# Score blocks of three groups in one stretch of 64-row work, with the second MoE product in 64-row halves between them

## The chip, the cores and the metric

The kernel runs on one core of a Trainium2 chip. The metric is the device time of one execution in microseconds. The engines are named as in the profile: PE is TensorE's matmuls and PEld its weight loads, DVE is VectorE, ACT is ScalarE, POOL is GpSimd, and SP is the engine whose queue issues DMAs here.

## The reference

A sliding-window attention is followed by a two-layer network with a squared ReLU. The batch is 8, there are 8 heads, 576 positions and a head dimension of 64; the window reaches 32 positions to either side.

```python
scores = scale * np.matmul(q, k.transpose(0, 1, 3, 2))
scores = np.where(np.abs(pos[:, None] - pos[None, :]) <= 32, scores, -1e9)
attn   = softmax(scores)
x = np.matmul(attn, v)          # as 4608 tokens x 512
h = x @ w_in                    # 512 x 2048
r = np.maximum(h, 0.0)
out = (r * r) @ w_out           # 2048 x 512, float32
```

## The kernel before

**Units of work.** The 4608 tokens are cut into 24 groups G of 192 queries (three groups, g = 0 to 2, for each batch b), and into 36 output blocks u of 128 tokens.

For a group, `scores` (S) multiplies k by q for all eight heads and for the two key windows w = 0 and 1. The head dimension is 64, so each matmul uses only 64 of the array's 128 rows: heads with an even number use rows 0 to 63, the odd ones rows 64 to 127, and they alternate. The sixteen matmuls of a group fill `AT`, 2048 columns in four PSUM banks. ACT takes the exponential of each half of AT (line 573), DVE multiplies it with a mask (line 578) into one of three `PT` buffers, `pv` (P) multiplies that with v (line 606) back into AT, and DVE divides and clears (lines 625 to 634). `xturn` transposes the result into `XT`, a ring of 1536 tokens, by DMA transposes on SP's queue (lines 701 and 704).

The first MoE product is `mm1` (A, line 721): 192, 256 or, from token 2048 on, 512 tokens at a time, by parts of the 2048 hidden features; ACT takes the relu out of the two PSUM tiles `HT` (line 727) and DVE the square into the ring `GT` (line 730). The second product is `mm2` (B, line 741): for a block u sixteen matmuls of 128 rows by 512 columns, in four segments, accumulate in `OUTP[u % 2]`; ACT evicts it (line 751) and stores it. The last block has a form of its own (`mm2_last`).

**Inputs.** Loads of q, k and v (`load_qk`, `load_v`, lines 378 and 427) go through POOL's queue and convert to bf16. From batch 2 on, q and k are transposed by DMAs on SP's queue (`turn_dma`, line 509), in chunks of 128 positions. Each load is recorded with `after=self.moe`: it waits for the score or first-product block that was recorded last before it.

**Order.** Nothing is emitted in the order of the code. `Prog.rec` collects operations with their dependences, an estimated duration and a key. One key unit is 64 tokens of the first product: A's key is its place in tokens, S of group G has 3G − `LEAD`, loads come a further `AHEAD` before, turns 3 units before S, and B of block u stands at 2u + `LAG`. The operations are recorded in the order of their keys. `Prog.schedule` then plays a list schedule: each engine takes, of the operations whose inputs are there by its estimates, the one with the lowest key. The DMA rings are played too, with an allowance (`slack`) added to the landing of each transfer. `Prog.emit` writes each engine's instructions in that order with the semaphore waits. On the chip each engine then works strictly in this order.

Of the kernel before, what the change touches and what calls it, by code (L numbers as in the profile page):

```python
# [18 lines left out]
RING = 1536  # L19
NV, NRAW = 6, 6  # L20
NTURN = 2
NXT = 3
LEAD = 13.0
LAG = 9.0
AHEAD = 9.0
TISS = 1340
# [37 lines left out]
PIECES = {"k": ((0, 1), (2, 3), (4,)), "q": ((0, 1), (2,), (3, 4))}  # L64
KC = ((0, 224), (224, 192), (416, 160))


class Op:
    __slots__ = ("eng", "fn", "deps", "order", "inc", "val", "sem", "dma", "dur", "key", "i",
                 "succ", "left", "ready", "start", "end", "lat", "move", "name", "slack")  # L70


class Prog:
# [5 lines left out]
    def __init__(self, nc):  # L79
        self.nc = nc  # L80
        self.ops = []
        self.writer = {}
        self.readers = {}

    def rec(self, eng, fn, reads=(), writes=(), dma=None, dur=100, key=0.0, move=0, name="", after=None, slack=0, war=()):
# [5 lines left out]
        op.slack = slack  # L91
        op.lat = self.LAT[eng]
# [24 lines left out]

    def schedule(self):
        ops = self.ops
        for op in ops:  # L120
            op.succ, op.left, op.ready = [], 0, 0
        for op in ops:
# [13 lines left out]
        order = ["POOL", "SP", "ACT"]  # L136
        now = spent = 0.0

        def done(op, end):
            for s in op.succ:  # L140
                s.ready = max(s.ready, end if op in s.deps or op.eng != s.eng else free[op.eng])
                s.left -= 1
                if not s.left:
                    heapq.heappush(wait[s.eng], (s.ready, s.i, s))
# [27 lines left out]
        while True:  # L172
            best = None
            for e in engs:
                if pool[e]:
# [13 lines left out]
            if serve(t):  # L189
                continue  # L190
            while wait[e] and wait[e][0][0] <= t:
                _, i, op = heapq.heappop(wait[e])
                heapq.heappush(pool[e], (op.key, i, op))
            first = pool[e][0]
# [10 lines left out]
            else:  # L205
                op.end = t + op.dur + op.lat
                done(op, op.end)
        assert len(out) == len(ops)
        self.length = max(o.end for o in out)
        at = free["PE"] = 1500  # L210
        for op in sorted((o for o in out if o.eng == "PE"), key=lambda o: o.start):
            gap = min(op.start, WARM, self.idle_end.start) - at
            one = 430 if at < 5000 else 230
            for k in range(int((gap - 60) // one)):
                w = Op()
                w.eng, w.fn, w.dma, w.deps, w.i = "PE", self.idle, None, {self.idle_on}, op.i
                w.inc, w.val, w.sem, w.start, w.end, w.dur, w.key = False, None, None, at + one * k, 0, one, -99
                w.name = "idle"
# [4 lines left out]
    def emit(self):  # L223
        nc = self.nc
        engs = {"PE": nc.tensor, "ACT": nc.scalar, "DVE": nc.vector, "POOL": nc.gpsimd, "SP": nc.sync}
        for op in self.ops:
            for d in op.deps:
                if d.dma is None and not (d.eng == "PE" and op.eng == "PE"):
                    d.inc = True
        sems = {e: nc.alloc_semaphore(f"s_{e}") for e in engs}  # L230
        count = {e: 0 for e in engs}
# [5 lines left out]
        for op in self.ops:  # L237
            e = engs[op.eng]
            need = {}
            for d in op.deps:  # L240
                if d.dma is None and d.eng == "PE" and op.eng == "PE":
                    continue
                need[d.sem] = max(need.get(d.sem, 0), d.val)
            for s, v in need.items():
# [26 lines left out]
class Gen:  # L271
# [5 lines left out]
    def alloc(self):  # L277
# [13 lines left out]
        self.E = [sb(f"e{i}", [128, 1024], BF16) for i in range(2)]  # L291
        self.PT = [sb(f"pt{i}", [128, 8, 128], BF16) for i in range(3)]
        self.RS = [sb(f"rs{i}", [128, 8], F32) for i in range(4)]
# [223 lines left out]
    def scores(self, G, ws):  # L517
        b, g = divmod(G, 3)
        i = b % 2
        kt, qt = self.KT[i], self.QT[i]  # L520
        key = 3 * G - LEAD + 0.3 * ws[0]
        a = 192 * g
# [38 lines left out]
        if G < NBIAS:  # L561
            rd += [t for w in ws for t in tags[w]]
        self.moe = self.p.rec("PE", f, reads=rd, writes=[t for w in ws for t in tags[w]], key=key, dur=190 + 235 * len(ws),
                              name=f"S{G}{'AB'[ws[-1]]}")
        for w in ws:
            n = 2 * G + w
            sc = self.AT[:, 1024 * reg[w]:1024 * reg[w] + 1024]
            e_, pt = self.E[n % 2], self.PT[n % 3]
            if G < NBIAS:
                self.p.rec("ACT", lambda e, pt=pt, sc=sc: e.activation(pt[:].rearrange("p h q -> p (h q)"), sc, ACTF.Exp, scale=0.125),  # L570
                           reads=tags[w], writes=[("pt", n % 3)], key=key, dur=act(1024), name=f"X{G}{'AB'[w]}")
                continue
# [5 lines left out]
            self.p.rec("DVE", lambda e, pt=pt, ee=ee, mb=mb: e.tensor_tensor(pt[:], ee, mb, ALU.mult),  # L578
                       reads=[("e", n % 2), ("mask", mi)], writes=[("pt", n % 3)], key=key, dur=dve(1024),
                       name=f"M{G}{'AB'[w]}")  # L580

    def pv(self, G, w):
# [5 lines left out]
        vt, pt, avp = self.V[G % NV], self.PT[n % 3], self.AT  # L588
        hi, lo = [self.half(2 * reg, x) + self.half(2 * reg + 1, x) for x in (1, 0)]


        def f(e):
            if w and G < NDUP:
                for h in range(8):
                    x, y = divmod(h, 4)
                    c = c0 + 512 * x + 65 * y
                    e.matmul(avp[:, c:c + 65], self.PT[(n - 1) % 3][:, 4 * (h % 2) + h // 2, :], vt[:, 0, h, 0:65], start=(y == 0),
                             stop=True, skip_group_check=True)
# [10 lines left out]

        rd = [("v", G % NV, w), ("vset", G % NV), ("pt", n % 3), "zz"]  # L610
        if G % 3 != 1:
# [3 lines left out]
        if G < NDUP and w:  # L615
            rd += [("pt", (n - 1) % 3), ("v", G % NV, 0)]
        self.p.rec("PE", f, reads=rd + (lo if w and G >= NDUP else []), writes=hi + lo, key=key, dur=260 + 160 * (w and G < NCLR) + 260 * (w and G < NDUP),
# [18 lines left out]
    def xturn(self, G):  # L636
        xa, xb = self.XA[G % 3], self.XB[G % 3]
        key = 3 * G - LEAD + 0.5
        r = 192 * G % RING
# [94 lines left out]
    def mm2(self, u, seg, key):  # L734
# [4 lines left out]
        def f(e):  # L739
            for d in range(4 * seg, 4 * seg + 4):  # L740
# [4 lines left out]
                       + ([f"outp{u % 2}"] if seg else []),  # L745
                       writes=[f"outp{u % 2}"], key=key, dur=864, name=f"B{u}.{seg}")
        if u == 1 and seg == 0 and not XTD:
            self.p.idle_end = o
# [34 lines left out]
    def build(self):  # L783
# [33 lines left out]
        for g in (1, 2, 4, 5):  # L817
            self.copy_v(g, K + 7 if g < 3 else 3 * g - LEAD - AHEAD)
        todo = []

        def at(key, f, *a):
            todo.append((key, len(todo), f, a))

        for G in range(NG):
            b, g = divmod(G, 3)
            if b > 1:
                key = 3 * G - LEAD - AHEAD
                for t in "kq":
# [3 lines left out]
                if g and G < NVR:  # L832
                    key = 3 * G - LEAD - 0.5 if G >= VCS else key
                    at(key + 0.01, self.copy_v, G, key - VKEY if G >= VCS else key)
            for t in "kq":
                key = 3 * G - LEAD - (0.6 if b < NTURN else 3)
                for c in (g,) if b < NTURN else PIECES[t][g]:
                    at(key, self.turn_pe if b < NTURN else self.turn_dma, t, b, c, key)
            for ws in ((0,), (1,)) if G < NSPLIT else ((0, 1),):
                at(3 * G - LEAD + 0.3 * ws[0], self.scores, G, ws)  # L840
# [58 lines left out]
```

## Time and profile before

| | us |
|---|---|
| median of 3 runs | 303.6 |
| lowest and highest | 303.34, 303.64 |
| profiled execution, span from its first to its last instruction | 301.1 |
| PE busy | 291.9 |
| PEld busy | 170.9 |
| DVE busy | 166.5 |
| ACT busy | 160.7 |
| POOL busy | 102.4 |

Of the profiled execution's own time the profile gives the span; the median of the runs is 2.5 us longer, for what lies around the span. The ends of matmuls are modelled, so their starts are what to read. A few matmul records are missing from the trace: a row of a timeline with x3 where its neighbours have x4 is as long as they are.

### The profile page before, as it was taken

Reading aid. Unit: us, or ns where it says so; the run is one execution under the profiler, and the core shown is the slowest. Engines: PE = TensorE matmul, PEld = TensorE weight load, DVE = VectorE, ACT = ScalarE, POOL = GpSimd, SP = SyncE. Lnnn points to the kernel's source line nnn. Section 1 sums busy time; section 2 is a strip of 40 time slices with the busy share of each in tenths; the row PEclk is TensorE's granted clock in tenths of the full one; section 3 lists DMA queues with packets and bytes.
Section 4 is the critical chain, followed back from the end, with each engine's and each line's share of the span. In section 5 each row is a group of like instructions: output and inputs, shape, how many; then the busy total and the mean of one; then the engine's idle time right before and its main releaser. Section 6 shows DMA issues by size and latency. Waiting matters only on the chain.

```text
span 301.1 us, 6232 instructions
## 1 busy us (share of the span) xinstructions
PE 291.9 (97%) x2394; PEld 170.9 (57%) x2431; DVE 166.5 (55%) x385; ACT 160.7 (53%) x250; POOL 102.4 (34%) x131
## 2 busy tenths in 40 slices
PE   7899999999999999999999999999999999999996
PEld 2578866846677777764444445445444444444445
DVE  5898785726766766664378756666456322222100
ACT  3587834826567646644656666455636443443312
POOL 8993335406543543654065454330000000000000
PEclk9999999999999999999999999999999999999999
DMA  9999999999998999999999999994121201000112
GB/s 167 176 206 183 196 178 176 168 163 208 175 158 138 141 160 191 147 157 177 199 152 135 166 162 143 199 168 101 54 50 49 60 35 37 35 35 36 37 70 105
DMA packets 160060, 39.83 MB, mean 132 GB/s; under 512 B 149408, under 2 KB 155552, under 8 KB 160032
## 3 DMA queue, kind: packets, MB, share of 16 engines
q0 software_dynamic: 105824, 17.93, 86.1%
q1 hardware_dynamic: 48880, 12.14, 28.4%
q10 hardware_dynamic: 5328, 9.37, 8.9%
q8 instruction: 19, 0.31, 0.4%
q14 instruction: 9, 0.07, 0.1%
HBM read 36.70 MB, written 9.44 MB: 153 GB/s over the span
## 4 chain that ended last, share of the span: by engine, by line
PE 87%; DMA 7%; POOL 3%; issue 1%; ACT 1%; DVE 0%; ACTq 0%; POOLq 0%
PE ht L721 41%; PE outp L741 38%; DMA w<-in_moe_w_in_dram 5%; PE at L606 4%; PE at L548 3%; DMA xt<-xa 2%; POOL v L427 1%; POOL w L440 1%; PE at L469 1%; PE ht L766 1%; PE outp L766 1%; POOL kpair L410 1%; POOL qpair L410 1%; ACT rt L727 0%; ACT oe L751 0%
## 5 line engine op out<-in xcount | busy, mean ns | idle before, releaser
L721 PE MATMUL ht<-xt,w 128*128 128x256 bf16 (+2 forms) x886 | 142.4, 302 | 1.7 <-DMA xt<-xa 0.5
L741 PE MATMUL outp<-w,gt 128*128 128x512 bf16 x535 | 134.3, 379 | 1.4 <-issue 0.2
L727 ACT ACTIVATE rt<-ht 128x512 bf16<-128x512 f32 (+1 forms) x152 | 86.4, 577 | 90.8 <-PE ht L721 85.7
L721 PEld LDWEIGHTS ht<-xt,w 128*128 128x128 bf16 x896 | 80.8, 98 | 43.8 <-DMA xt<-xa 1.0
L730 DVE TENSOR_TENSOR gt<-rt 128x512 bf16<-128x512 bf16 (+1 forms) x152 | 61.3, 408 | 65.0 <-ACT rt L727 63.2
L741 PEld LDWEIGHTS outp<-w,gt 128*128 128x128 bf16 x560 | 52.3, 98 | 56.0 <-ACT oe L751 1.1
L378 POOL DMA_DIRECT2D kraw<-in_k_dram x30 | 25.3, 850 | 95.2 <-PE at L548 76.5
L573 ACT ACTIVATE e<-at 128x1024 bf16<-128x1024 f32 x46 | 44.8, 1021 | 11.2 <-PE at L548 11.1
L578 DVE TENSOR_TENSOR pt<-e,mask 128x1024 bf16<-128x1024 bf16 x46 | 31.5, 691 | 24.7 <-ACT e L573 24.6
L427 POOL DMA_DIRECT2D v<-in_v_dram x48 | 38.4, 822 | 0.0
L751 ACT ACTIVATE oe<-outp 128x512 f32<-128x512 f32 x35 | 21.1, 602 | 24.1 <-PE outp L741 24.1
L378 POOL DMA_DIRECT2D qraw<-in_q_dram x30 | 25.5, 860 | 0.0
L606 PEld LDWEIGHTS at<-v,pt 128*128 128x128 bf16 x384 | 18.0, 98 | 10.0 <-DVE at L634 1.8
L606 PE MATMUL at<-v,pt 128*128 128x65 bf16 x384 | 20.1, 194 | 0.5 <-ACT pt L570 0.5
L628 DVE TENSOR_TENSOR xb<-at,rs 128x512 bf16<-128x512 f32 x24 | 16.6, 690 | 1.1
L628 DVE TENSOR_TENSOR xa<-at,rs 64x512 bf16<-64x512 f32 x24 | 16.7, 695 | 0.8
L548 PEld LDWEIGHTS at<-qt,kt 64*128 64x128 bf16 x384 | 10.8, 94 | 8.3 <-issue 7.5
L548 PE MATMUL at<-qt,kt 64*128 64x128 bf16 x384 | 15.2, 217 | 0.1
L625 DVE RECIPROCAL rs<-at 64x8 f32<-64x8 f32 (+1 forms) x48 | 10.0, 209 | 9.5 <-PE at L606 7.8
L634 DVE MEMSET at<- 64x520 f32 x23 | 11.3, 492 | 3.7 <-DVE xa L628 2.9
L434 DVE COPY v<-v 64x512 bf16<-64x512 bf16 x16 | 5.8, 366 | 6.9 <-PE ht L721 5.8
L773 DVE COPY oe<-ht 128x128 f32<-128x128 f32 x1 | 0.3, 291 | 14.7 <-PE ht L766 14.7
(67 smaller groups left out, 82.1 us busy)
## 6 DMA issues: line engine op xcount, KB each, us to landing
out_dram<-oe ACTq DMA_DIRECT2D x35, 256.0 KB, 3.8
kraw<-in_k_dram POOLq DMA_DIRECT2D x24, 128.0 KB, 5.6
qraw<-in_q_dram POOLq DMA_DIRECT2D x24, 128.0 KB, 5.9
w<-in_moe_w_in_dram POOLq DMA_DIRECT2D x4, 512.0 KB, 10.6
v<-in_v_dram POOLq DMA_DIRECT2D x16, 128.0 KB, 7.3
w<-in_moe_w_out_dram POOLq DMA_DIRECT2D x4, 512.0 KB, 18.9
v<-in_v_dram POOLq DMA_DIRECT2D x16, 96.0 KB, 6.7
v<-in_v_dram POOLq DMA_DIRECT2D x16, 64.0 KB, 5.8
```

The source lines that it names most:

```text
L378: self.p.rec("POOL", lambda e: e.dma_start(raw[0:n, x % 2, :].rearrange("p (h d) -> p h d", h=8), s), writes=[("raw", t, x // 2, x % 2)], ...
L427: self.p.rec("POOL", lambda e, j=j, lo=lo, hi=hi, k0=k0: e.dma_start(vt[lo - k0:hi - k0, j, :, 0:64], self.v[b, :, lo:hi, :].rearrange("h ...
L548: mm = e.matmul(sc[:, 512 * par + 128 * j:512 * par + 128 * j + 128], kt[r:r + 64, j, k0:k0 + 128], q, start=G >= NBIAS, stop=True, skip_g ...
L573: self.p.rec("ACT", lambda e, e_=e_, sc=sc: e.activation(e_[:], sc, ACTF.Exp, scale=0.125), reads=tags[w], writes=[("e", n % 2)], key=key, ...
L578: self.p.rec("DVE", lambda e, pt=pt, ee=ee, mb=mb: e.tensor_tensor(pt[:], ee, mb, ALU.mult), reads=[("e", n % 2), ("mask", mi)], writes=[( ...
L606: mm = e.matmul(avp[:, c:c + 65], pt[:, 4 * (h % 2) + h // 2, :], vt[:, w, h, 0:65], start=(w == 0 and y == 0), stop=True, skip_group_chec ...
L628: self.p.rec("DVE", lambda e: e.tensor_tensor(x[r0:128, :].rearrange("p (x y c) -> p x y c", x=2, y=4), av[:, :, :, 0:64], rb, ALU.mult), ...
L721: mm = e.matmul(ht[:, n * x:n * x + n], self.W1[:, ft, 128 * d:128 * d + 128], self.XT[:, ft, r:r + n], start=(ft == 0), stop=(ft == 3))
L727: self.p.rec("ACT", lambda e: e.activation(rt[:, 0:c], ht[:, 0:c], ACTF.Relu), reads=[f"ht{k % 2}"], writes=[("rt", k % 4)], key=key, dur= ...
L730: self.p.rec("DVE", lambda e: e.tensor_tensor(gt[:, d0:d0 + len(ds), r:r + n], rr, rr, ALU.mult), reads=[("rt", k % 4)], writes=[("gt", s, ...
L741: mm = e.matmul(op[:], gt[:, d, r:r + 128], self.W2[:, d, :], start=(d == 0), stop=(d == 15))
L751: self.p.rec("ACT", lambda e: e.activation(oe, op[:], ACTF.Copy), reads=[f"outp{u % 2}"], writes=[("oe", u % 4)], key=key, dur=act(512), n ...
```

## The change

For batches 5, 6 and 7 (groups 15 to 23) the three score blocks of a batch are put on PE as one unbroken chain, with two half blocks H between them: S(G), H0, S(G+1), H1, S(G+2). The two H together are the second product of two whole output blocks u and u+1. H0 multiplies, for each of the 16 parts of the hidden features, rows 0 to 63 for block u and rows 64 to 127 for block u+1; H1 does the other two halves. Each H has 32 matmuls of 64 rows by 512 columns. Each accumulates into OUTP[u % 2] and OUTP[(u+1) % 2] at once, and H1 waits by a semaphore for the end of H0 (`fence`).

In the planner, the first S of a chain is taken when the inputs of all three groups are known to be there within 500 ns, and when two blocks u and u+1 are found that have not begun, whose inputs are there and whose PSUM tiles are free or will be within 500 ns (`fill`); the eight B operations of these blocks are then dropped (`dead`). Until this is so, other work with a higher key goes first. A chain is taken without H (its S then stand singly) when the first product has come to 6 units before the first group's own place, or 20 us after its inputs were there.

`PT` gets seven buffers for three. The keys move for all groups: LEAD 13 to 14, LAG 9 to 9.5, AHEAD 9 to 9.5, and `SOONER` shifts loads and turns of batches 4 to 7. Groups in a chain have their keys 0.75 units apart in place of 3, so their loads, turns and xturn come earlier by up to some 5 units.

```diff
-LEAD = 13.0
-LAG = 9.0
-AHEAD = 9.0
+LEAD = 14.0
+LAG = 9.5
+AHEAD = 9.5
...
+NPT = 7
+CHAINS = {15: 3, 18: 3, 21: 3}
+CSTEP = 0.75
+CEARLY = 12.0
+CHOLD = 12.0
+CLAST = 6.0
+READY = 500
+PATIENCE = 20000
+SOONER = {4: (1, 1.5), 5: (-1.5, 1), 7: (-0.5, 1.5), 6: (2, 2)}
...
     def schedule(self):
...
+        def known(deps, t):
+            return all(d.end is not None and d.end <= t + READY for d in deps)
...
+        def fill(op, t):
+            u = min((u for u, b in self.blocks.items() if b[0].end is None), default=None)
+            if u is None or u + 1 not in self.blocks:
+                return None
+            both = self.blocks[u] + self.blocks[u + 1]
+            deps = {d for b in both for d in b.deps | b.order if d not in both}
+            if not known(deps, t):
+                return None
...
+            seq = [ops[0], op.chain[1], ops[1]] + op.chain[2:]
...
+            return seq
...
+                    if op.chain:
+                        if known({d for y in op.chain for d in y.data}, t):
+                            run = fill(op, t) or []
+                            op.since = t if op.since is None else op.since
+                        if run or at >= op.urge + CHOLD - CLAST or op.since is not None and t > op.since + PATIENCE:
+                            break
+                    elif not (op in opens and any(at >= h[2].urge for h in held if h[2].chain) and spare(t) < 3):
+                        break
...
     def emit(self):
...
+            for d in op.fence:
+                need[d.sem] = max(need.get(d.sem, 0), d.val)
...
     def scores(self, G, ws):
-        key = 3 * G - LEAD + 0.3 * ws[0]
+        key = self.pos(G) - LEAD + 0.3 * ws[0]
...
-            e_, pt = self.E[n % 2], self.PT[n % 3]
+            e_, pt = self.E[n % 2], self.PT[n % NPT]
...
+    def half_block(self, u, kind):
+        gt, w2 = self.GT, self.W2
+        def f(e):
+            for d in range(16):
+                for x in range(2):
+                    v = u + (x + kind) % 2
+                    r, r0 = 128 * v % RING, 64 * x
+                    mm = e.matmul(self.OUTP[v % 2][:], gt[r0:r0 + 64, d, r:r + 128], w2[r0:r0 + 64, d, :], start=kind == 0 and d == 0,
+                                  stop=kind == 1 and d == 15, skip_group_check=True)
+            return mm
+        return f
+
+    def pos(self, G):
+        x = self.chained.get(G, 0)
+        return 3 * (G - x) + CSTEP * x
+
+    def chain(self, G0, n):
+        ops = [self.scores(G0 + x, (0, 1)) for x in range(n)]
+        ops[0].chain, ops[0].urge = ops, 3 * G0 - CHOLD
+        for x in range(n):
+            for w in range(2):
+                self.pv(G0 + x, w)
+            self.xturn(G0 + x)
 
     def pv(self, G, w):
-        key = 3 * G - LEAD + 0.3 * w + 0.1
-        reg = 1 if NBIAS <= G < NSPLIT or G < NDUP and w else 0
+        key = self.pos(G) - LEAD + 0.3 * w + 0.1
+        reg = self.chained[G] % 2 if G in self.chained else 1 if NBIAS <= G < NSPLIT or G < NDUP and w else 0
...
     def build(self):
...
+            pos = self.pos(G)
             if b > 1:
-                key = 3 * G - LEAD - AHEAD
+                key = pos - LEAD - AHEAD - SOONER.get(b, (0, 0))[0]
...
-                key = 3 * G - LEAD - (0.6 if b < NTURN else 3)
+                key = pos - LEAD - (0.6 if b < NTURN else 3 + SOONER.get(b, (0, 0))[1])
...
+            if G in self.chained:
+                if G in CHAINS:
+                    at(3 * G - CEARLY, self.chain, G, CHAINS[G])
+                continue
```

More of the change, by code (lines that the diff above doesn't have):

```diff
@@ L65 @@
 KC = ((0, 224), (224, 192), (416, 160))
+NPT = 7
[7 more added lines that the diff above has]
+SOONER = {4: (1, 1.5), 5: (-1.5, 1), 7: (-0.5, 1.5), 6: (2, 2)}
 class Op:
     __slots__ = ("eng", "fn", "deps", "order", "inc", "val", "sem", "dma", "dur", "key", "i",
-                 "succ", "left", "ready", "start", "end", "lat", "move", "name", "slack")
+                 "succ", "left", "ready", "start", "end", "lat", "move", "name", "slack", "chain", "inner", "dead",
+                 "data", "urge", "since", "fence")
 class Prog:
@@ L91, in rec @@
         op.slack = slack
+        op.chain, op.inner, op.dead, op.data, op.urge, op.since, op.fence = None, False, None, (), None, None, ()
         op.lat = self.LAT[eng]
@@ L137, in schedule, with spare @@
         now = spent = 0.0
+        run, at = [], -99.0
+        opens = {b[0] for b in self.blocks.values()}
+        def known(deps, t):
+            return all(d.end is not None and d.end <= t + READY for d in deps)
+        def spare(t):
+            n = 0
+            for u in sorted(self.blocks):
+                both = self.blocks[u]
+                if both[0].end is None:
+                    if not known({d for b in both for d in b.deps if d not in both and d.eng != "ACT"}, t):
+                        return n
+                    n += 1
+            return n
+        def fill(op, t):
[6 more added lines that the diff above has]
+                return None
+            ops = []
+            for kind in range(2):
+                h = Op()
+                h.eng, h.fn, h.dma, h.deps, h.order, h.i, h.key = "PE", self.half_block(u, kind), None, set(), set(), op.i, op.key
+                h.inc, h.val, h.sem, h.dur, h.lat, h.name = False, None, None, 3450, op.lat, f"H{u}.{kind}"
+                h.succ, h.left, h.ready, h.end, h.dead, h.chain, h.fence = [], 0, 0, None, None, None, ()
+                ops.append(h)
+            ops[1].fence = ops[:1]
+            ops[0].deps = deps
+            for b in both:
+                b.dead = ops[1]
+            ops[1].succ = both
+            op.dur = 560
+            seq = [ops[0], op.chain[1], ops[1]] + op.chain[2:]
+            for x in op.chain[1:]:
+                x.inner, x.dur = True, 450
+            seq[-1].dur += 100
+            return seq
         def done(op, end):
@@ L174, in schedule @@
             for e in engs:
-                if pool[e]:
+                while pool[e] and pool[e][0][2].dead:
+                    heapq.heappop(pool[e])
+                while wait[e] and wait[e][0][2].dead:
+                    heapq.heappop(wait[e])
+                if e == "PE" and run:
+                    if run[0].left:
+                        continue
+                    t = max(free[e], run[0].ready)
+                elif pool[e]:
                     t = free[e]
@@ L226, in emit @@
         for op in self.ops:
+            op.deps = {d.dead or d for d in op.deps}
             for d in op.deps:
@@ L819, in build @@
         todo = []
+        self.chained = {G + x: x for G, n in CHAINS.items() for x in range(n)}
+        p.half_block = self.half_block
         def at(key, f, *a):
```

80 lines of the change are left out of this document (63 added, 17 removed).

## The prediction

> **What bounds the kernel now.** I read the page first (busy time, slices, chain), then the groups by line, the stages, the waits, and the timeline around one score block.
>
> ```profile
> span 301.1 us, 6232 instructions
> PE 291.9 (97%) x2394; PEld 170.9 (57%) x2431; DVE 166.5 (55%) x385; ACT 160.7 (53%) x250; POOL 102.4 (34%) x131
> PE 87%; DMA 7%; POOL 3%; issue 1%; ACT 1%; DVE 0%; ACTq 0%; POOLq 0%
> 24.00:72.00 48.00, 47.18 (x510) 34.21 (x515) 31.06 (x72) 27.73 (x46) 18.62 (x24) 1.00 1.83 181
> 140.00:172.00 32.00, 31.58 (x231) 15.38 (x234) 21.65 (x46) 19.20 (x30) 15.20 (x19) 1.00 1.64 161
> 200.00:230.00 30.00, 29.68 (x211) 14.45 (x214) 16.17 (x36) 16.79 (x26) 0.00 (x0) 1.00 0.43 71
> PE ht L721 <- DMA xt<-xa: 0.5, 1, 0.5
> ```
>
> TensorE is busy 97% of the span and makes up 87% of the chain that ended last. In the three stages (columns: stretch, its length, then busy us of PE, PEld, DVE, ACT, POOL, the granted clock, DMA share, GB/s) it lacks 0.8 us between 24 and 72 us, 0.4 us between 140 and 172, and 0.3 us between 200 and 230, at a clock of 1.00. DVE and ACT are half empty. After the opening the longest wait of TensorE for another unit is one of 0.5 us. So from about 24 us on, a microsecond taken off TensorE's queue is a microsecond off the span, as long as nothing new holds the queue; and work moved between other engines is worth nothing. The change edits TensorE's queue in batches 5 to 7 (score blocks of groups 15 to 23, those from 148.8 to 226.5 us), so I look at one such block, S18, with its neighbours:
>
> ```profile
> 173.12 1.03 PE L741 MATMUL outp<-w,gt 128*128 128x512 bf16 x4
> 173.98 1.03 PE L721 MATMUL ht<-xt,w 128*128 128x512 bf16 x3
> 174.85 1.03 PE L741 MATMUL outp<-w,gt 128*128 128x512 bf16 x4
> 175.81 0.62 PE L548 MATMUL at<-qt,kt 64*128 64x128 bf16 x16
> 176.36 1.04 PE L721 MATMUL ht<-xt,w 128*128 128x512 bf16 x4
> 177.23 1.03 PE L741 MATMUL outp<-w,gt 128*128 128x512 bf16 x4
> 178.09 1.03 PE L721 MATMUL ht<-xt,w 128*128 128x512 bf16 x4
> 178.96 0.42 PE L606 MATMUL at<-v,pt 128*128 128x65 bf16 x8
> 179.22 1.02 PE L741 MATMUL outp<-w,gt 128*128 128x512 bf16 x4
> L548 PE MATMUL at<-qt,kt x384: 212/216/227, 9.7 to 226.9; 64*128 64x128 bf16 x192
> L548 PEld LDWEIGHTS at<-qt,kt 64*128 64x128 bf16 x384 | 10.8, 94 | 8.3 <-issue 7.5 <-ACT qt L497 0.4 <-DVE gt L730 0.2
> ```
>
> A row's second number runs to the modelled end of its last matmul, so the starts are what to read. Four 512-column matmuls take 0.86 us from start to start whatever line follows (177.23 to 178.09): 0.216 each, and a change of line or of output costs nothing. (One row shows x3 for lack of a record; its length is that of four.) Only the score block is different. From 174.85 to its start are 0.96 us, 0.10 more than four matmuls need; to the start of the next block are 0.55 us. Inside it sixteen matmuls of 128 columns on 64 rows start within 0.62 less one duration of 0.216, so every (0.62 − 0.216) / 15 = 0.027 us, two per 0.054, which is what 128 columns take at 0.216 for 512: both halves of the array run at once, and their weight loads (94 ns each, 10.8 / 384 = 28 ns of unshared time) keep up. At that rate the block needs 16 × 0.027 = 0.43 us. It takes 0.10 + 0.55 = 0.65, and the block after it another 0.01 (0.87 for 0.86). So entering and leaving 64-row work costs 0.65 + 0.01 − 0.43 = 0.23 us per block.
>
> **The change, part by part.**
>
> *Switches.* Nine score blocks in batches 5 to 7 now pay 9 × 0.23. Chained as S, H, S, H, S with the H also on 64 rows, a batch enters and leaves once: six of nine switches go, 6 × 0.23 = 1.36 us, all of it on TensorE's queue. This is the one term that is there by design.
>
> *Half blocks.* Per chain, blocks u and u+1 (32 matmuls of 128 rows, 32 × 0.216 = 6.91 us) become two H of 32 matmuls of 64 rows by 512 columns. No row shows these. Nearest is the score block itself: 0.027 us for 128 columns is 0.108 for 512, 32 × 0.108 = 3.46 per H, 6.91 for two: no difference, and I take that. Two bounds above it: if of each pair of weight loads one step of 0.027 were exposed, 96 pairs (3 chains × 2 × 16) would cost 2.6 us; if a full load of 0.094, 9.0 us. Below zero I see nothing: TensorE already runs a column per 0.42 ns in both shapes.
>
> Here the Trainium skill speaks against the change (TensorE: Matmul & The Clock Gate, Part 3, "What overlaps and what doesn't"): a weight load overlaps matmuls in flight only when its row group differs, which would make every pair wait for its loads. The trace does not bear it out for the score block, at 0.027 us per matmul with 94 ns loads; by the page the sum would end at the 9.0 us above, not at zero. The same page (Part 3, "Measured speedup vs the span model") has four row tiles of 512 columns at 3.07 times, not 4; the score block's two tiles run at the full factor of two.
>
> *The fence between the two H.* H1 starts only when H0's last matmul has signalled; behind that wait stand H1, the last score block and everything later on TensorE. ACT started 0.04 us after a recorded matmul end (rows below: 176.43, which is 175.81 + 0.62, then 176.47), and a 512-column matmul is recorded with 0.38 us, so the signal is there about 0.42 us after the last start; S(G+1) between them covers 0.22 + 0.43 = 0.65. Cost nothing; uncovered, as when that block goes first, up to 0.2 × 3 = 0.6.
>
> *Waits for ACT inside a chain.* S(G+1) overwrites the PSUM that S(G)'s two exponentials read.
>
> ```profile
> 175.91 0.60 ACT L751 ACTIVATE oe<-outp 128x512 f32<-128x512 f32 x1 [0.21 <-PE outp L741]
> 176.47 1.02 ACT L573 ACTIVATE e<-at 128x1024 bf16<-128x1024 f32 x1
> 177.39 1.02 ACT L573 ACTIVATE e<-at 128x1024 bf16<-128x1024 f32 x1
> 178.29 0.60 ACT L727 ACTIVATE rt<-ht 128x512 bf16<-128x512 f32 x1
> 177.52 0.69 DVE L578 TENSOR_TENSOR pt<-e,mask 128x1024 bf16<-128x1024 bf16 x1 [1.36 <-ACT e L573]
> 178.44 0.69 DVE L578 TENSOR_TENSOR pt<-e,mask 128x1024 bf16<-128x1024 bf16 x1 [0.22 <-ACT e L573]
> ```
>
> They end at 178.41, 2.60 us after the block's start. H0 covers 0.43 + 3.46 = 3.89 us, so even two more items of 0.60 ahead on ACT (3.80) stay hidden. After the chain the cover is thinner: two evictions (0.60 each) and two exponentials (0.92 apart), 3.0 us of ACT, stand before the relu of the next MoE blocks. TensorE has two first-product blocks for the two free PSUM tiles (1.73), then second-product blocks of u+2 once the first eviction is over. I take nothing; with no block ready it is 3.0 − 1.7 = 1.3 per chain, 3.9 in all. On DVE six masks (0.69 each, 4.1 us) fall into the 8.2 us of a chain, fewer than it has free. The second-product values (P, 0.26 us from 178.96 to 179.22) and the division and clearing behind them keep their count and place on DVE; the seven pt buffers, more than the six a chain fills, mean that no mask waits for P.
>
> *Loads, turns and the planner's keys.* Key units pass at (175.81 − 148.79) / 9, 3.0 us each, counting S15 to S18. Before, every load of group G is issued behind S(G−3), 9 units ahead.
>
> ```profile
> 148.79 0.62 PE L548 MATMUL at<-qt,kt 64*128 64x128 bf16 x16
> POOL kraw L378 <- PE at L548: 76.5, 14, 10.1
> 35.00 1.75 POOL L378 DMA_DIRECT2D kraw<-in_k_dram  x2 [10.06 <-PE at L548]
> kraw<-in_k_dram POOLq DMA_DIRECT2D x24, 128.0 KB, 5.6
> kt<-kraw SPq DMA_TRANSPOSE x30, 5.3
> ```
>
> A chained batch asks for 16 loads on POOL in 1.5 units instead of 6, at some 0.88 us (1.75 for two) 14 us of issuing, then 5.6 to land, then ten turns on SP and 5.3 to land: about 29 us if four turns of 1.2 are left at the end. The first loads lie 8 units (31 − 23), 11.5 and 9 ahead of the chain's key, 24 to 35 us, and 16 or more (39 − 23) ahead of the key at which it is forced. It is planned no earlier than its data, and MoE work takes its place while it slips; the six xt transposes of a batch come earlier by up to 5.5 units, and who waits for them, the first product, gains slack. I cost this at nothing. If a chain stood at the queue's head with a late transpose, all of TensorE would stand behind it.
>
> *The opening.* The lead grows for all groups. A load's gate is the last score or first-product block before its key; with keys at 3G − 23.5 instead of 3G − 22 the loads of group 6 fall behind S2 instead of S3, those of 8 and 9 behind first-product blocks. So POOL's 10.06 us pause before 35.00 and its like go, and DMA gets these loads up to 10 us sooner. What may gain or lose is one place:
>
> ```profile
> 59.08 0.69 DVE L628 TENSOR_TENSOR xa<-at,rs 64x512 bf16<-64x512 f32 x1
> 58.00 3.99 SPq L509 DMA_TRANSPOSE kt<-kraw  x2
> 62.04 7.25 DMA xt<-xa
> 69.33 0.94 PE L721 MATMUL ht<-xt,w 128*128 128x256 bf16 x7 [0.53 <-DMA xt<-xa]
> xt<-xa SPq DMA_TRANSPOSE x21, 5.9
> ```
>
> xa was ready at 59.77, but SP stood behind two k turns until 62, and the transpose landed 7.25 us later: TensorE's 0.53 us. Turns that are done earlier free SP (−0.5 at best, all that there is); a fuller DMA could lengthen the transpose again by 7.25 − 5.9 = 1.35. Between −0.5 and +1.4 I take 0, since both act on the same wait.
>
> **The sum.** Of the profiled execution the span is given, 301.1; the median of 303.6 adds 2.5 around it, which nothing here touches. 301.1 − 1.3 = 299.8 of span (six switches, rounded down from 1.36 for the joints inside a chain, which no row shows), and 299.8 + 2.5 = 302.3.
>
> **The rivals.**
>
> - *Half blocks below full rate (slower).* The place is the 96 pairs of H. For it: each 64-row matmul needs its own load, and the halves accumulate in two PSUM banks at once, which score blocks, that only overwrite, never did. Against it: the 0.027 us. It decides from 1.36 / 96 = 14 ns per pair, 6% over 0.216. At 0.027 per pair: 302.3 + 2.6 = 304.9; at 0.094: 311.3. The weight-load rule cited above is this rival. Chance 0.12.
> - *A chain that holds the queue (slower).* Late data at its head, or no MoE work ready behind it: 1.3 per chain, 302.3 + 3.9 = 306.2; it decides from 0.45 per chain. For it: SP and POOL get a batch at once. Against: room to slip by 8 units and DVE and ACT half empty. Chance 0.08.
> - *No effect.* The planner finds no two whole blocks with their data and lets the scores go singly, or the opening gives back 1.4: 303.6. For it: two blocks must be untouched and the last one evicted. Against: the second product trails the first by 9.5 units, more than the 8 of a 512-token tile. Chance 0.13.
> - *The opening gains too.* 302.3 − 0.5, with joints at nothing: 301.7. Chance 0.05.
>
> The forecast itself keeps 0.62, at 302.3, from 301.7 to 303.0 by the opening's bounds.
>
> **How the numbers follow.** A measurement tells 0.2%, 0.6 us. Faster by more is the forecast and the last rival, 0.67; within it "no effect", 0.13; slower the first two, 0.20. The range begins at 301.5 (six switches, 0.5 in the opening, 0.2 of scatter) and goes up to 305.0, to take in the first rival's lower price; what is left out is its dear end and the held queue, under 0.15.
>
> **What would show it.** In the profile after: three stretches where L548 blocks alternate with rows of a new line on 64*128 128x512, 3.46 us from the first start to the next block's; a joint of 0.00 to 0.03 between them; 0.10 before each stretch and 0.12 after it. Wrong would be: a pair above 0.23 us; a gap on TensorE between the blocks of a chain, released by ACT or by PE; TensorE idle behind a chain, waiting for ACT; L548 blocks that stand alone after 148 us; more than 0.5 us of waiting for xt between 60 and 75 us.

## The result, and the profile after

The changed kernel takes 315.92 us (median of 6 runs, 313.52 to 318.50) against 303.3 for the kernel before: a ratio of 1.0395, 95% interval 1.0365 to 1.0424. By that ratio it is 12 us slower (12.6 by the medians), where 1.3 us faster was forecast. Here and below, medians and ranges are of all runs, ratios and their intervals of the runs in the faster of two states, which leaves out the odd run more than 1.5% above the kernel's fastest. The profiled execution took 313.52 us with a span of 311.7, 10.6 more than before.

From the page of the changed kernel: span, busy time, the clock and DMA in forty slices, the chain that ended last, the group of the new half blocks, and the landing of loads.

```profile
span 311.7 us, 6433 instructions
PE 294.5 (94%) x2494; PEld 172.7 (55%) x2527; DVE 164.7 (53%) x385; ACT 161.0 (52%) x250; POOL 102.5 (33%) x131
PE   7899999999699949999799999999999999999997
PEclk9999999999989988999999999999999999999999
DMA  9999999999999999999999489992104100110012
PE 62%; DMA 24%; POOL 8%; issue 4%; SPq 0%; DVE 0%; ACT 0%; POOLq 0%
L707 PE MATMUL outp<-w,gt 64*128 64x512 bf16 x192 | 21.7, 376 | 0.0
L707 PEld LDWEIGHTS outp<-w,gt 64*128 64x128 bf16 x192 | 9.1, 94 | 10.0
kraw<-in_k_dram POOLq DMA_DIRECT2D x24, 128.0 KB, 22.6
v<-in_v_dram POOLq DMA_DIRECT2D x16, 128.0 KB, 22.8
```

TensorE is no longer the whole chain: DMA has 24% of it (7% before) and POOL 8% (3%). A load of k lands 22.6 us after its issue, where 5.6 were enough before. The stages say when, and the waits of TensorE for whom (first the kernel before from 72 to 140 us, then four stages of the changed kernel):

```profile
72.00:140.00 68.00, 67.32 (x660) 47.78 (x669) 44.38 (x98) 40.59 (x62) 32.48 (x41) 1.00 1.84 161
```

```profile
24.00:72.00 48.00, 47.34 (x511) 34.28 (x515) 30.80 (x71) 27.75 (x47) 29.84 (x37) 1.00 1.77 179
72.00:140.00 68.00, 60.48 (x589) 43.19 (x595) 40.94 (x90) 36.72 (x57) 32.05 (x40) 0.95 1.78 159
140.00:172.00 32.00, 29.57 (x255) 14.96 (x255) 13.91 (x29) 15.63 (x22) 4.50 (x6) 1.00 1.78 167
172.00:200.00 28.00, 27.74 (x247) 14.14 (x248) 17.03 (x38) 15.73 (x25) 13.05 (x16) 1.00 1.35 133
```

```profile
PE ht L864 <- DMA xt<-xa: 6.2, 2, 4.0
PE at L749 <- DVE pt L693: 2.5, 1, 2.5
```

From 72 to 140 us TensorE lacks 7.5 us (0.7 before), from 140 to 172 another 2.4 (0.4 before); from 172 to 200, where the second chain stands, 0.3. The wait of the second stage is at 150 us, and the first chain begins at 161.7. All of the loss lies before the first chain. The first of the long waits, in the timelines of TensorE and of DVE and in the chain that ended last:

```profile
79.46 1.67 PE L884 MATMUL outp<-w,gt 128*128 128x512 bf16 x7
83.66 0.42 PE L749 MATMUL at<-v,pt 128*128 128x65 bf16 x8 [2.53 <-DVE pt L693]
83.91 4.44 PE L884 MATMUL outp<-w,gt 128*128 128x512 bf16 x12
```

```profile
82.50 0.29 DVE L547 COPY v<-v 64x512 bf16<-64x512 bf16 x1 [3.54 <-DMA v<-in_v_dram]
82.82 1.29 DVE L693 TENSOR_TENSOR pt<-e,mask 128x1024 bf16<-128x1024 bf16 x2
```

```profile
50.82 31.65 DMA v<-in_v_dram
```

A load of v issued at 50.82 landed 31.65 us later, at 82.47. (In the kernel before, the same load was issued at 71.67 and landed at 78.50: issued 21 us sooner, it came 4 us later.) DVE's queue had the copy of v at its head and waited 3.54 us; the masks stood behind it, P behind the masks, and TensorE behind P. After such a wait it also runs slowly: the twelve matmuls from 83.91 to 88.19 take 4.28 us where 2.59 are due (0.216 each), with a granted clock of 0.50 from 85 to 87 us (the slices of PEclk with an 8 are this wait and the one at 112 us). The mean clock of 0.989 stands for some 3.4 us of the span. The Trainium skill (TensorE: Matmul & The Clock Gate, Part 1, "What's actually happening") has the half clock follow an idle window of about 3.4 us; here an idle time of 2.5 us was enough. The idle time of 2.16 us before 152.09 cost no clock: the matmuls behind it start every 0.216 us.

The last long wait, by the chain that ended last:

```profile
120.15 22.78 DMA qraw<-in_q_dram
142.94 1.27 SPq L622
144.30 7.43 DMA xt<-xa
152.09 0.81 PE ht L864 x3
```

A load of q for batch 5, the first chained one, took 22.78 us; the turn that waited for it stood on SP's queue in front of the transpose of xt, and the first product waited for that. So TensorE's direct waits are 6.2 us for xt, behind late loads on SP's queue, and 2.5 us for the masks, behind a late load on DVE's queue.

The chain itself did what was forecast. First chain, timelines of TensorE and ACT:

```profile
160.76 1.03 PE L864 MATMUL ht<-xt,w 128*128 128x512 bf16 x3
161.72 0.62 PE L661 MATMUL at<-qt,kt 64*128 64x128 bf16 x16
162.17 3.62 PE L707 MATMUL outp<-w,gt 64*128 64x512 bf16 x32
165.63 0.61 PE L661 MATMUL at<-qt,kt 64*128 64x128 bf16 x16
166.07 3.62 PE L707 MATMUL outp<-w,gt 64*128 64x512 bf16 x32
169.53 0.61 PE L661 MATMUL at<-qt,kt 64*128 64x128 bf16 x16
170.30 1.67 PE L864 MATMUL ht<-xt,w 128*128 128x512 bf16 x7 [0.16 <-issue]
```

```profile
162.52 1.94 ACT L688 ACTIVATE e<-at 128x1024 bf16<-128x1024 f32 x2
```

The row at 170.30 holds seven of eight matmuls and is 1.67 us long where a whole one is 1.89: the record of its first is missing, so it began 0.216 us sooner and its idle time of 0.16 is none. Score blocks inside take 0.45 and 0.44 us, an H takes 3.46 (162.17 to 165.63), entry costs 0.10 (160.76 to 161.72 is 0.96 for four matmuls), the last score block with the exit 0.55 (169.53 to 170.08), and the two exponentials end at 164.46, 1.2 us before the next score block wants their PSUM.

### The profile page after: what moved, and what is told of

Read it like the earlier page. It is cut to its first block, busy times and chain, and to the rows that moved or that the text cites. A ratio compares the mean times of both kernels' runs of the same rounds, so it can differ in the third digit from the quotient of the medians.

```text
span 311.7 us, 6433 instructions
## 1 busy us (share of the span) xinstructions
PE 294.5 (94%) x2494; PEld 172.7 (55%) x2527; DVE 164.7 (53%) x385; ACT 161.0 (52%) x250; POOL 102.5 (33%) x131
## 4 chain that ended last, share of the span: by engine, by line
PE 62%; DMA 24%; POOL 8%; issue 4%; SPq 0%; DVE 0%; ACT 0%; POOLq 0%
PE ht L864 29%; PE outp L884 20%; DMA v<-in_v_dram 10%; DMA qraw<-in_q_dram 7%; PE outp L707 7%; DMA w<-in_moe_w_in_dram 4%; POOL v L540 3%; PE at L749 2%; DMA xt<-xa 2%; PE at L661 2%; POOL kraw L491 2%; POOL qraw L491 1%; POOL w L553 1%; PE ht L910 1%; POOL qpair L523 1%
## 5 line engine op out<-in xcount | busy, mean ns | idle before, releaser
L864 PE MATMUL ht<-xt,w 128*128 128x256 bf16 (+2 forms) x883 | 140.8, 304 | 7.8 <-DMA xt<-xa 6.2
L884 PE MATMUL outp<-w,gt 128*128 128x512 bf16 x446 | 112.0, 384 | 1.1 <-issue 0.2
L884 PEld LDWEIGHTS outp<-w,gt 128*128 128x128 bf16 x464 | 43.9, 99 | 48.0 <-issue 1.8
L749 PEld LDWEIGHTS at<-v,pt 128*128 128x128 bf16 x384 | 18.1, 99 | 12.6 <-issue 4.4
L707 PE MATMUL outp<-w,gt 64*128 64x512 bf16 x192 | 21.7, 376 | 0.0
L707 PEld LDWEIGHTS outp<-w,gt 64*128 64x128 bf16 x192 | 9.1, 94 | 10.0
## 6 DMA issues: line engine op xcount, KB each, us to landing
kraw<-in_k_dram POOLq DMA_DIRECT2D x24, 128.0 KB, 22.6
v<-in_v_dram POOLq DMA_DIRECT2D x16, 64.0 KB, 22.6
```

The source lines that it names most:

```text
L707: mm = e.matmul(self.OUTP[v % 2][:], gt[r0:r0 + 64, d, r:r + 128], w2[r0:r0 + 64, d, :], start=kind == 0 and d == 0, stop=kind == 1 and d ...
L749: mm = e.matmul(avp[:, c:c + 65], pt[:, 4 * (h % 2) + h // 2, :], vt[:, w, h, 0:65], start=(w == 0 and y == 0), stop=True, skip_group_chec ...
L864: mm = e.matmul(ht[:, n * x:n * x + n], self.W1[:, ft, 128 * d:128 * d + 128], self.XT[:, ft, r:r + n], start=(ft == 0), stop=(ft == 3))
L884: mm = e.matmul(op[:], gt[:, d, r:r + 128], self.W2[:, d, :], start=(d == 0), stop=(d == 15))
```

## The experiments

The edits are shown cut to what they change; several settings may stand on one line.

**First round: keys or chains?** Theory 1: the keys moved for all groups unhook the loads from the score block three groups back. Theory 2: the chains, which want three groups at once.

```diff
-LEAD = 14.0; LAG = 9.5; AHEAD = 9.5; SOONER = {4: ..., 5: ..., 7: ..., 6: ...}
+LEAD = 13.0; LAG = 9.0; AHEAD = 9.0; SOONER = {}
```

> The changed kernel with the keys of the kernel before (LEAD 13, LAG 9, AHEAD 9, no SOONER) and the chains kept. Theory 1 (the moved keys unhook the loads of q, k and v from the score block three groups back; they pile up in POOL's DMA queue, land late, and hold DVE's and SP's queues and so TensorE): no long stall before 140 us, chains as in the changed kernel, 302 to 303 us, since the six saved switches are worth 1.4 us; up to 2 us more if the three groups of a chained batch loaded at once pile up too. Theory 2 (the chains themselves, whose batches load, turn and transpose three groups at a time, make the stalls): 309 us or more.

Measured 310.7 us (1.023, 1.019 to 1.027): between 24 and 140 us no wait of TensorE is over 0.6 us, but there is one of 2.2 us at 143 and more from 197 to 250, around chains that the planner itself puts at 159, 197 and 237 us. Neither theory alone. And the run is no clean test: the planner's own length for it is 315.1 us (301.6 for the changed kernel), and only the chain at 197 has its half blocks; by the trace the score blocks of the other two stand singly.

```diff
-CHAINS = {15: 3, 18: 3, 21: 3}
+CHAINS = {}; SOONER = {}
```

> The changed kernel without chains and without SOONER: only LEAD 14, LAG 9.5, AHEAD 9.5 and the seven pt buffers are left of the change. Theory 1: the stalls at 72 to 140 us stay, load landing stays near 20 us, 312 to 317 us (the loss without the 1.4 us that the chains save). Theory 2: 303 to 304 us, landing near 6 us.

Measured 320.45 us (1.0576, 1.052 to 1.0632), k landing after 21.5 us. Without any chain the loss is larger than with them: theory 2 falls for the early waits. The planner's own length is 303.1 us here, 17 less than was measured.

```diff
-    after=self.moe                 # loads of q, k, v
+    o.deps.add(self.sop[G - 3])    # the score block of group G-3, batches 2 to 7
```

> The changed kernel with all its keys and chains, but every load of q, k and v of group G from batch 2 on waits for the score block of group G-3, as the loads of the kernel before do, in place of the last score or first-product block recorded before it. Theory 1: the stalls go with the gate, landing back near 6 us, 302 to 304 us. If instead the greater lead itself (order of TensorE's queue) makes the stalls: 309 us or more.

Measured 328.81 us, far from the forecast of theory 1, and yet its stage is as that theory has it: from 72 to 140 us TensorE lacks nothing and k lands in 5.4 us. The loss moved behind the second and third chain; the score blocks of the first stand singly (the stage, then rows of TensorE's timeline from the last score block of the second chain on):

```profile
72.00:140.00 68.00, 68.00 (x674) 48.20 (x672) 45.40 (x99) 40.51 (x62) 31.72 (x40) 1.00 1.89 158
```

```profile
212.72 0.61 PE L664 MATMUL at<-qt,kt 64*128 64x128 bf16 x16
214.54 0.41 PE L753 MATMUL at<-v,pt 128*128 128x65 bf16 x8 [1.21 <-issue]
215.41 0.43 PE L753 MATMUL at<-v,pt 128*128 128x65 bf16 x8 [0.46 <-ACT e L692]
222.25 0.62 PE L753 MATMUL at<-v,pt 128*128 128x65 bf16 x8 [2.39 <-DVE at L781]
226.48 1.01 PE L868 MATMUL ht<-xt,w 128*128 128x512 bf16 x2 [3.61 <-DMA xt<-xb]
```

A batch's loads now wait for the chain before, so each chain comes so late that the first product has no tokens left, and the P blocks, with nothing to fill between them, wait for DVE, then the first product for xt. That is the planner's doing in full view: its own plan is 329.3 us long here.

```diff
-AHEAD = 9.5
+AHEAD = 9.0
```

> The changed kernel with AHEAD 9.0 in place of 9.5, one number: loads of batches 2 and 3 then have keys equal to that of the score block three groups back and wait for it again; those of batches 4 to 7 are still moved by SOONER. Theory 1: the waits at 72 to 90 us go, those at 110 and 148 us may stay, 303 to 309 us, clearly below the changed kernel. Theory 2: no change, 313 us or more.

Measured 327.08 us, a miss: the same late chains (planned length 324.4, the first again without half blocks), with SOONER still piling up loads (k 11.9 us).

**Second round: what is it about the loads?** The planner's landing times and the chip's, worked out from the order and the trace (no. of the load on POOL's queue from 0, times in us; the planned times hold an allowance of 5 us):

```
                        before               changed
load                issued  planned  landed  issued  planned  landed
no. 77, end batch 4  114.4   124.9   120.0    97.4    108.1   120.6
no. 93, end batch 5  141.3   151.8   147.9   127.3    129.9   147.7
no. 109, end batch 6 170.1   179.6   176.3   153.6    151.3   172.3
```

The change issued the last load of batch 5 14 us sooner, and it landed at the same time. Before, the chip was 3 to 5 us ahead of the plan; now it is 12 to 21 us behind, and every queue is ordered for landings that do not happen. From no. 41 to no. 77 a load lands every 1.66 us ((120.6 − 61.0) / 36) where the plan has 1.27. In the kernel before, whose loads never piled up, it is 1.60 over the same loads, and from 72 to 140 us 41 loads landed there and 43 in the changed kernel, at 161 and 159 GB/s: a queue that was never empty delivered no faster. So theory 3: DMA is full, and its rate, not the gate, is what loads wait for.

```diff
-AHEAD = 9.0    # against the kernel before: only this, and seven pt buffers
+AHEAD = 9.5
```

> No chains, no SOONER, LEAD 13 and LAG 9 as before; of the moved keys only AHEAD 9.5 in place of 9 is left (and the seven pt buffers). Theory 3: half a unit is enough to put each load behind another block than the score block three groups back, the loads pile up, landing near 20 us, 310 to 320 us. If LEAD or LAG makes the loss of the changed kernel: 303 to 304 us.

Measured 315.25 us (1.0395, 1.0365 to 1.0426), k 18.0 us. Half a unit alone makes a loss as large as that of the whole change (the seven buffers are in the next run too, which loses nothing).

```diff
-AHEAD = 9.5    # against the run without chains and SOONER above: only this
+AHEAD = 9.0
```

> No chains, no SOONER, LEAD 14 and LAG 9.5 as in the changed kernel, but AHEAD 9: the run that lost most without chains with one number put back. Theory 3: the loads wait for the score block three groups back again, landing near 6 us, 303 to 305 us. If the longer lead makes the loss: 312 us or more.

Measured 302.53 us (0.9978, 0.9962 to 0.9994): 17.9 us under the run with AHEAD 9.5 (320.45). The longer lead costs nothing, and is even a little faster. The landing of k, with AHEAD 9.5 and with 9:

```profile
kraw<-in_k_dram POOLq DMA_DIRECT2D x24, 128.0 KB, 21.5
kraw<-in_k_dram POOLq DMA_DIRECT2D x24, 128.0 KB, 5.3
```

```diff
-  vt[...], self.v[b, :, lo:hi, :]                    # load_v
+  vt[..., 0:HV if b > 1 else 8, ...], self.v[b, 0:HV if b > 1 else 8, lo:hi, :]
+HV = 4    # then 1
```

> The changed kernel, every instruction in the same order on every engine, but from batch 2 on only four of the eight heads of v are loaded, which leaves that part of v out of the result: one sixth fewer bytes and packets of load. Theory 3: DMA is the limit, its backlog drains, landings come back towards the planned times, and the waits between 72 and 150 us go: 302 to 306 us. If it is the order of the loads in the queue or the order of TensorE's blocks that makes the waits: 311 us or more.

> The changed kernel, same order on every engine, but from batch 2 on only one of the eight heads of v is loaded, which leaves the others out of the result: 7/24 fewer load bytes, where half of v was 4/24. Theory 3: the backlog is gone or nearly so, landings by the plan, 302 to 305 us, less than with half of v. If the half of v only saved what its own DMAs took: about 307 us.

Measured 310.1 us (309.33 to 310.84; 1.022, 1.0192 to 1.0249) with half of v and 305.85 (304.33 to 307.90; 1.0089, 1.0062 to 1.0115) with an eighth; k lands after 17.9 and 14.7 us. The stage from 72 to 140 us, where the changed kernel lacks 7.5 us of TensorE, with half of v (5.9) and with an eighth (3.7):

```profile
72.00:140.00 68.00, 62.09 (x614) 45.06 (x621) 43.25 (x97) 37.88 (x58) 31.37 (x40) 0.97 1.76 156
```

```profile
72.00:140.00 68.00, 64.32 (x630) 45.40 (x629) 44.35 (x97) 38.09 (x58) 30.12 (x41) 0.97 1.76 156
```

With every instruction in its place, bytes (and packets with them) taken off the loads take 5.8, then 10.1 of the 12.6 us away. From no. 41 to no. 77 a load lands every 1.57 and 1.37 us, where it was 1.66. I had expected more from the half: the backlog shrank, it did not vanish.

> The changed kernel with all three chains and all its keys, but the loads of batches 2 to 4 wait for the score block four groups back, and so go out in the order of the groups and one group sooner than in the kernel before. Theory 3 (DMA is full; no order of the queue brings the data of batch 5 sooner): no waits up to about 120 us, landings by the plan there, late ones from batch 5 on with waits before the first chain; 304 to 311 us, between the kernel before and the changed one. If overtaking and the pile alone made the loss: 302 to 303 us. If neither: 313 us or more.

```diff
-    after=self.moe                 # loads of batches 2 to 4
+    o.deps.add(self.sop[G - 4])
```

Measured 314.22 us (1.0378, 1.0295 to 1.0461), in the range that I had kept for neither reason, with waits of TensorE already from 69 us, though its planned length is 301.7. The trace has the pile again: k lands after 17.2 us, and the landings fall behind the plan by 8 us in batch 3 and by 16 at the end of batch 5. In the changed kernel the loads of group 8 overtake those of group 7, since their gate is an early first-product block; here they go out in order, and nothing is gained. So the loss needs no overtaking, and one group sooner is already too soon; I had not expected the first batches to feel it.

The planner's own length, the latest end in the order that `Prog.schedule` makes when the kernel is built, sorts the runs. In the first four rows the loads of the batches without chains wait for the score block three groups back, and the plan is within 4.5 us of the measured time, long or short:

```
(us)                          planned  measured
kernel before                  302.7    303.3
LEAD 14, LAG 9.5, AHEAD 9      303.1    302.5
old keys, three chains         315.1    310.7
gate S(G-3), three chains      329.3    328.8
changed kernel                 301.6    315.9
its keys, no chains            303.1    320.5
AHEAD 9.5 alone                302.9    315.3
gate S(G-4), batches 2 to 4    301.7    314.2
```

In the last four, where loads are asked for sooner, it is 12 to 17 us too short. So the chains with old gates lose what the planner itself says; the changed kernel loses what the planner does not know.

**Third: a chain without the moved loads.**

```diff
+LEAD = 13.0; LAG = 9.0; AHEAD = 9.0; CHAINS = {21: 3}; SOONER = {6: (1, 1), 7: (1, 1)}
+after=self.moe1    # loads of batches 6 and 7: last first-product block; keys 3 apart
```

> Keys of the kernel before (LEAD 13, LAG 9, AHEAD 9) and only the chain of batch 7, whose data are in before it is wanted; the loads of batches 6 and 7 keep their spread of 3 units per group, one unit sooner, and wait for the last first-product block instead of a score block. Theory 3 (the chain saves two switches each, 0.45 us; all of the loss comes from asking DMA for loads sooner than it can deliver them): 0.3 to 0.5 us under the kernel before, near 303.0, and no wait over 0.6 us after 24 us. If a chain costs something of its own: 303.5 or more.

Measured 304.92 us (302.35 to 307.16 over 12 runs; 1.0022, 0.999 to 1.0054): inconclusive. The median is where a chain with a cost of its own was expected, the interval includes no change. The profiled execution, span 300.2, keeps within the forecast 0.6 us per wait (the longest after 24 us is 0.5, for a turned q at 157 us), but the runs scatter by 5 us; moving the gate of two batches made k land after 7.4 us.

> The kernel without chains and with AHEAD 9, LEAD 14, LAG 9.5 once more, so that the next one is compared with it on the same chip: 302.5 us, all theories alike.

Measured 302.56 us (302.38 to 303.05; 0.9976, 0.9964 to 0.9988).

```diff
+AHEAD = 9.0; CHAINS = {21: 3}; SOONER = {7: (0, 2)}    # LEAD 14, LAG 9.5; load keys 3 apart
```

> The kernel above with the chain of batch 7 alone; its loads keep their spread of 3 units per group and so wait for the score block three groups back, its turns come 2 units sooner. Theory 3: two switches less, 0.45 us under the run above, 302.1 us, and steady from run to run. If a chain needs its loads sooner even here or its half blocks cost time: as the run above or more.

Measured 302.62 us (301.83 to 303.90): the lowest single run of all, but no lower median than the run without a chain (302.56), which is what was expected if a chain has a cost. Its timeline has the saving:

```profile
207.48 1.03 PE L864 MATMUL ht<-xt,w 128*128 128x512 bf16 x4
208.44 0.62 PE L661 MATMUL at<-qt,kt 64*128 64x128 bf16 x16
208.90 3.62 PE L707 MATMUL outp<-w,gt 64*128 64x512 bf16 x32
212.35 0.61 PE L661 MATMUL at<-qt,kt 64*128 64x128 bf16 x16
212.79 3.62 PE L707 MATMUL outp<-w,gt 64*128 64x512 bf16 x32
216.25 0.61 PE L661 MATMUL at<-qt,kt 64*128 64x128 bf16 x16
216.79 1.90 PE L864 MATMUL ht<-xt,w 128*128 128x512 bf16 x8
```

From the end of the last full-width block (208.34 by four times 0.216) to 216.79 are 8.45 us for two H (6.91) and three score blocks: 1.54 for the three, 1.55 with what the block behind them takes longer, where three lone blocks need 3 × 0.66 = 1.98. So 0.43 us per chain on TensorE; in the runs' times it is within their scatter and not shown.

```diff
+AHEAD = 9.0; CHAINS = {18: 3, 21: 3}; SOONER = {6: (3, 2), 7: (3, 2)}    # load keys 3 apart
```

> The kernel above with the chain of batch 6 too, and loads and turns of batches 6 and 7 sooner by 3 and 2 units. Theory 3: the first chain must wait for the third group's data while its first group's tokens come due, the waits eat the 0.45 us and more: 303 to 306 us. If chains are free wherever they stand: 301.7 us.

Four runs of 303.22, 304.63, 308.15 and 311.99 us: no interval, but none below the run without chains (302.38 to 303.05). What a second chain is worth is not shown by it, for only the chain of batch 6 has half blocks; the score blocks of batch 7 stand singly, as in the kernel before:

```profile
226.82 0.62 PE L661 MATMUL at<-qt,kt 64*128 64x128 bf16 x16
227.37 2.76 PE L884 MATMUL outp<-w,gt 128*128 128x512 bf16 x12
230.07 0.62 PE L661 MATMUL at<-qt,kt 64*128 64x128 bf16 x16
```

The planner's own length is 304.4 us, against 302.6 with the chain of batch 7 alone.

## Why the prediction was wrong

*Right:* the switch cost and the term of 1.3 us on TensorE's queue (0.43 per chain measured, 1.3 for three); half blocks at full rate (3.46 us, no joint above 0.02); the fence at nothing; ACT hidden by H (1.2 us to spare) and no wait behind a chain (P at 171.81 in its place). The rule of the Trainium skill on weight loads (TensorE: Matmul & The Clock Gate, Part 3, "What overlaps and what doesn't") is not borne out by the half blocks either: their loads of 94 ns stay hidden. Both slower rivals I had named, half blocks below full rate and a chain that holds the queue, did not happen in the changed kernel; behind the late chains of the run with the gate S(G−3) the second did, where P waited up to 2.39 us for DVE.

*Wrong:* the step "Loads, turns and the planner's keys", which I cost at nothing, and "The opening", which I bounded at +1.4 us. I saw that the loads would be unhooked from S(G−3) and read POOL's waits, 76.5 us in all, as slack to be used. They were the pacing. The page before showed it in the DMA row, which I did not quote:

```profile
DMA  9999999999998999999999999994121201000112
```

That is nine tenths or more in 26 of the first 27 slices. A batch's 16 loads take 26.6 us at 1.66 us each, and TensorE needs 27 us for a batch (9 units of 3.0): DMA had next to no time to give (of the time from 60 to 175 us, 7 us in all had no load under way, and none in the changed kernel). So the loads came no sooner, some even later, while the planner, whose DMA is faster under a pile (1.27 us per load) than the chip's, put scores, copies, masks and turns where they could not yet run. I had limited the effect to one transpose at 62 us; it came from 72 to 150 us, 6.2 us through xt behind late k and q on SP's queue and 2.5 us through v on DVE's.

*Right in a part:* the −0.5 us that I saw in the opening fits what is seen when the gate is kept. The 0.53 us wait for xt at 69 us, the longest of the kernel before after 24 us, is gone in the two runs with LEAD 14, AHEAD 9 and no chain, which are 0.5 and 0.8 us faster than the kernel before; that the one makes the other was not tried apart from LAG.

*The sum of the loss.* Against the stages before, TensorE lacks 6.8 us more from 72 to 140 (7.5 less 0.7) and 2.0 more from 140 to 172 (2.4 less 0.4); the clock costs some 3.4, of which a part lies in the same waits; the chains give 1.3 back. That is 10.9 for the 10.6 us of span.

*Open:* with an eighth of v 2.7 us of loss remain (305.85 against 303.1 for the kernel before beside it), and k still lands after 14.7 us; what holds the rate at 1.66 us per load was not tried (most packets are under 512 B, and the transposes share the engines). Why runs with a chain scatter more than those without, even with paced loads, is open too.

The fastest version by its median is the one without chains, LEAD 14, LAG 9.5, AHEAD 9: 302.5 us, 0.2% under the kernel before (0.9978 and 0.9976).

## What to carry to other kernels

A wait on a queue that feeds DMA may be the kernel's pacing, not slack: before a load is moved sooner, compare what DMA must move per stage with what it moved there, and if it is full, the load will land no sooner. A planner's order is only as good as its rates; compare its planned times with the trace, transfer by transfer, because a model that is right behind a gate can be wrong behind a pile. Look into the trace of a variant for what its edit asks for: in four runs the planner left chains without their half blocks. Merging 64-row work into one stretch saved 0.2 us per switch on TensorE's queue here, too little to show in the runs' times, and no run here shows that moving loads for its sake pays.

## What was not expected of the hardware

Issuing far ahead has a limit of its own: in the changed kernel no load is issued with more than 20 others under way on POOL's queue. From 37 to 90 us each of the 21 issues that POOL came to late follows the landing of an older load by 0.30 to 0.33 us (36.95 and 37.28, 38.27 and 38.57, 82.47 and 82.78), with 15 to 19 under way, and POOL's queue stands still in between. What is counted there, loads or packets, the runs do not tell.

The transposes on SP's queue suffered far less than the loads from the pile on POOL's: xt lands after 6.8 and 7.0 us (5.9 and 4.7 before), loads of k after 22.6 (5.6). The Trainium skill (DMA: Bandwidth & Descriptors, "Queues, rings and completion order") has each DMA engine take turns between queues packet by packet, and the two medians agree with that.
